# Seven of eight experts put in order of their token count, with their sort moved forward, and more warming products at the start

## The chip, the cores and the metric

The kernel runs on one core of a Trainium2 chip. The metric is the device time of one execution in microseconds. Before the change three runs took 249.92, 250.83 and 251.06 us, so the median is 250.83 us.

The core has a matrix engine (PE, with its weight loads shown apart as PEld), a vector engine (DVE), a scalar engine (ACT), GpSimd (POOL, which also issues the indirect DMAs that gather and scatter rows) and a queue for direct DMAs (SP). Each engine works through its own list of instructions in order; the lists wait for one another through semaphores.

## The reference

A Mamba-2 scan is followed by a mixture of experts with one expert per token. Cut to what matters:

```python
# scan: 4 batches x 8 heads, 768 tokens, head_dim 32, d_state 16, chunks
y_intra = einsum((C B^T) * exp(cum_i - cum_j) * causal, x)
y_inter = einsum(C, state) * exp(cum)
state   = decay_full * state + sum_j B_j x_j exp(cum_last - cum_j)

x = attn_out.transpose(0, 2, 1, 3).reshape(3072, 256)
expert_idx = argmax(cosine(x, expert_emb) / tau)      # 8 experts
gate_w     = softmax(...)[expert_idx]
for e in range(8):                                    # w1: 256 x 1024, w2: 1024 x 256
    mask = expert_idx == e
    out[mask] = gate_w[mask] * (relu(x[mask] @ w1[e]) @ w2[e])
```

Everything is fp32. With the given inputs the eight experts receive 408, 348, 366, 396, 382, 354, 405 and 413 tokens, in this order of expert numbers (counted from the reference).

## The kernel before, in words

**The scan.** The sequence is cut into six chunks of 128 tokens (`NC`), each with all four batches and eight heads. `mamba` writes the order of all instructions out by hand (`manual_schedule`). Ahead of its loop stand the loads of the first chunks, constants, and products of a matrix of ones whose result nobody reads (`warm_up`). In chunk 0 and 1 the PE does, in turn, `inner` (L401), `outputs` (L439), `first_outputs` (L452), `sums` (L369) and `spread_decays` (L215); ACT keeps the outputs (`keep_outputs`, L464). The finished rows of each chunk, with their eight router scores, are sent to a table in HBM, `y_rows`.

**Routing.** `pick`, `count_picks`, `rank_rows` and `places` give every token its expert and its rank among that expert's tokens. `locate` (L743) turns this into sums over chunks, and `table` (L764, L766) turns the sums into a table of token numbers: for each of the eight experts four columns (`NT`) of 104 rows (`TR`), so at most 416 tokens. `from_rows` (L791) makes the indices `gi` for the gathers, `to_rows` with `out_rows` (L799, L1085 to L1095) the rows `to` for the scatters.

**Experts in order of count.** Every expert is a `Job`. The number of token columns that its products work on is fixed when the kernel is built. The first `FIXED` = 2 experts, numbers 0 and 1, have the full 416. The other six (`SORTED`) are put in order of their counts by `sort_experts`, some sixteen DVE instructions (L809 to L839, then L791 to L1095), and the i-th of them gets `CAPS[i]` columns: 416, 408, 400, 388, 376, 364. Tokens above a job's columns would be done by a loop at the end (`leftover`), which is skipped when there are none. Since the order is known only on the chip, `load_weights` reads the number of the expert from `k.order` into a register of SP (L94) for a sorted expert, and issues five DMAs: four for `w1` (L85) and one for `w2` (L105). Tiles for weights exist three times (`wp`, bufs=3).

**Between scan and experts** (`scan_end`). Expert 0 is done in two halves of 208 columns. The first half (`first`) holds tokens of the first three chunks and is gathered early, while the scan still runs; its eight steps `up(0)` to `up(7)` and the two `down` fill the PE while the routing of the last chunk is done on DVE. The second half is `late`, expert 1 is `whole`. `whole` gets its first two gathered tiles from an early table `gi0` and the other two from `gi`. `late` and `whole` share the tile `next_x` (six parts), and `Gates` squares their rows (ACT, L1417), takes a root on POOL (`power`, L1423) and makes the gate weights.

**The experts** (`moe`). From expert 1 on, `up_blocks` and `down_blocks` do the two products with one level of a Winograd scheme: 28 matmuls each (seven products of half-sized blocks, L1272 and L1344), each over half of the job's columns. The sums of blocks of weights (`sum_w1` L1229, `sum_w2` L1237) and of inputs (L1241) are on DVE. Between the two, the next job's rows are transposed (`turn_x`, L1171). The last job has `up_blocks` but plain `down` products (`moe_end`, L1202): 16 over a fixed half of 208 columns, 16 over the rest. Everything is a list per engine; a wait of one engine moves all that stands behind it.

The lines that the change touches most:

```python
def load_weights(k, e, parts=(0, 1), after=None):
    if e >= FIXED:
        i = bass.ds(nc.values_load(k.order[0:1, e - FIXED : e - FIXED + 1], engines=(SP,), ...), 1)
```

Of the kernel before, what the change touches and what calls it, by code (L numbers as in the profile page):

```python
# [17 lines left out]
Q = 128  # L18
# [5 lines left out]
KD, KF = DM // 128, F // 128  # L24
TR, NT = 104, 4
CAP = TR * NT
FIXED = 2
SORTED = E - FIXED
CAPS = [CAP - 8 * i - 4 * max(i - 2, 0) for i in range(SORTED)]
LEFT = (T - CAPS[-1]) // Q + E  # L30
# [594 lines left out]
def place_consts(k):  # L625
    nc, ints = k.nc, k.ints
    k.place_at = ints("place_at", [128, TR], [[1, TR]], 1, 0)
    k.first_of = ints("first_of", [128, NT], [[TR, NT]], 0, 0)
    k.idx_t = k.mc.tile([128, TR], F32, name="idx_t")
    k.same = k.mc.tile([128, E * NT], F32, name="same")  # L630
    nc.gpsimd.tensor_copy(out=k.same[:], in_=k.ident[:, 0:32])
    for b in range(1, NB):
        nc.gpsimd.tensor_tensor(
            out=k.same[:], in0=k.same[:], in1=k.ident[:, 32 * b : 32 * b + 32], op=ALU.add
        )
    k.minus = k.mc.tile([128, 1], F32, name="minus")
    nc.gpsimd.memset(k.minus[:], -1.0)
    k.shifted = k.mc.tile([128, E], F32, name="shifted")
    nc.gpsimd.memset(k.shifted[:], 0.0)
    nc.gpsimd.memset(k.shifted[0:1, 0:2], 1.0)  # L640


def pick(k, c):
# [123 lines left out]
    return t  # L767


def end_places(k, whole):  # L770
    nc = k.nc
    n = k.pz[1][:, 456 : 456 + E]
    nc.tensor.matmul(n, lhsT=k.ones[:], rhs=k.pre[:, NU, :], start=True, stop=True)
    t = table(k)
    k.gi = k.const.tile([TR, E * NT], I32, name="gi")
    k.to = k.const.tile([TR, E * NT], I32, name="to")
    from_rows(k, t[:, 0 : FIXED * NT], 0)
    late = late_job(k)
    gather_tiles(k, whole.x[:, HT:], k.gi, NT + HT)
    nc.vector.tensor_copy(out=k.idx[:], in_=t)  # L780
    idx = k.idx[:, 0 : FIXED * NT]
    to_rows(k, idx, 0)
    late.to, whole.to = k.to[:, HT:NT], k.to[:, NT : 2 * NT]
    k.n = k.const.tile([128, E], F32, name="n")
    nc.vector.tensor_copy(out=k.n[:], in_=n)
    return late


# [55 lines left out]
def mamba(k):  # L844
    nc = k.nc
    k.f = k.mc.tile([128, 2, Q], F32, name="f")
    k.fe = k.mc.tile([128, 2, 3], F32, name="fe")
    k.rT = k.mc.tile([128, 2, 2, 128], F32, name="rT")
    k.V = k.mc.tile([128, NB, 2 * D], F32, name="V")
    k.ends = k.mc.tile([128, 8, NB, 3], F32, name="ends")  # L850
    k.rr, k.wm = {}, {}
    for c in range(NC):
        k.ld[c] = Net()
        k.ld[c].g = []
    load_decays(k)
    expert_emb(k)
    load(k, 0, ("ct", "bi", "x"))
    build_consts(k)
    warm_up(k, 12)
    decays(k)  # L860
    load(k, 1, ("ct",))
    load(k, 0, ("b", "xa"))
    load(k, 1, ("bi", "x", "xa", "b"))
    square_emb(k)
    clear_first_half(k, 0)
    clear_first_half(k, 1)
    route_consts(k)
    spread_decays(k, 0)
    spread_decays(k, 1, [t[:, 384:512] for t in k.py + k.pz])
    warm_up(k, 1, 384)  # L870
    split_b(k, 0)
    inverses(k, 0, 0)
    scale_c(k, 0)
    inverses(k, 0, 1)
    block_ends(k)
    scale_emb(k)
    inner(k, 0, 0)
    mask_inner(k, 0, 0)
    turn_inverses(k, 0, k.py[0][:, 0:256])
    scale_x(k, 0, nc.gpsimd)  # L880
    scale_first_half(k, 0, nc.gpsimd)
    spread_ends(k, k.pz[0][:, 0:96])
    turn_emb(k, k.py[0][:, 256:272])
    scale_c(k, 1)
    steps = between(k, 1, NC)
    next(steps)

    for c in range(NC):
        t = k.ld[c]
        n = c + 1  # L890
        if c == 0:
            load(k, 2, ("ct", "x", "xa", "b", "bi"))
        elif c + 2 < NC:
            load(k, c + 2, ("x",))
        if 2 <= c < NC - 1:
            spread_decays(k, n)
        if 2 <= c < NC - 1:
            add_sums(k, c)
        if c >= 2:
            inner(k, c, 0)  # L900
        if c == NC - 1:
            finish(k, c - 1, (0,))
            early_places(k, c - 3)
        if c >= 2:
            mask_inner(k, c, 0)
        if c == NC - 2:
            load_first_w1(k, 0, t.masked)
        if c > 0 and c + 2 < NC:
            load(k, c + 2, ("ct",), t.masked if c >= 2 else None)
        if 3 <= c < NC - 1:  # L910
            finish(k, c - 1, (0,))
            locate(k, c - 3)
            keep_located(k, c - 3)
        if n < NC:
            scale_x(k, n, nc.gpsimd, t.paired if c >= 2 else None)
        if 1 <= c < NC - 1:
            scale_c(k, n)
        if c == 1:
            decay_states(k, 1)
            add_sums(k, c)  # L920
        if c >= 2:
            pick(k, c - 2)
        if c > 0:
            finish(k, c - 1, (2,) if c == NC - 1 else (1, 2) if 3 <= c else (0, 1, 2))
            keep_rows(k, c - 1)
            if c < NC - 1:
                send_rows(k, c - 1)
        inner(k, c, 1)
        mask_inner(k, c, 1)
        if c > 0 and n < NC:  # L930
            decay_states(k, n)
        if c > 0 and c + 2 < NC:
            load(k, c + 2, ("bi", "xa"), t.masked)
        if c == 0:
            sums(k, 0)
        if n < NC:
            split_b(k, n)
            mask_c(k, n)
            if c == 0:
                next(steps)  # L940
            pass_c(k, n)
        if c == NC - 1:
            k.early_x = half_rows(k)
            gather_tiles(k, k.early_x, k.gi0, 0, 3 * NB * Q)
        if c >= 2:
            count_picks(k, c - 2)
        if c == NC - 1:
            add_located(k, c - 3)
        if c == 0:
            scale_first_half(k, n, nc.gpsimd, (0,))  # L950
        elif n < NC:
            scale_first_half(k, n, nc.gpsimd, after=t.paired)
        if 3 <= c < NC - 1:
            add_located(k, c - 3)
        if c > 0:
            from_states(k, c)
        if c >= 2:
            rank_rows(k, c - 2)
            keep_ranks(k, c - 2)
        outputs(k, c, 0)  # L960
        if c == 0:
            inner(k, 1, 0)
            add_sums(k, 0)
            mask_inner(k, 1, 0)
        first_outputs(k, c, 0)
        for zs in ((0,), (1,)) if c == NC - 1 else (range(KD),):
            outputs(k, c, 1, zs)
            if c == 0:
                spread_decays(k, 2)
            first_outputs(k, c, 1, zs)  # L970
            keep_outputs(k, c, zs)
        if c > 0 and c + 2 < NC:
            load(k, c + 2, ("b",), t.kept)
        if c == NC - 2:
            load_first_w1(k, 1, t.kept)
        if c == NC - 1:
            hold(k, send_rows(k, c - 1), t.kept)
            load_weights(k, 0, (1,), t.kept)
        if c + 2 < NC:
            sums(k, n)  # L980
        if c == 2:
            turn_inverses(k, 1, k.pz[0][:, 0:256])
        if c == NC - 1:
            pick(k, c - 1)
            count_picks(k, c - 1)
        if c >= 2:
            places(k, c - 2)
        if c == 4:
            shift_places(k)
        if c == 1:  # L990
            inverses(k, 1, 0)
            inverses(k, 1, 1)
        if c == 0:
            scale_first_half(k, n, nc.gpsimd, (1,))
            place_consts(k)


def scan_end(k):
# [9 lines left out]
    pick(k, c)  # L1008
    count_picks(k, c)
    whole = whole_job(k)  # L1010
    gather_tiles(k, whole.x[:, 0:HT], k.gi0, NT, 3 * NB * Q)
    for f in range(3):
        first.up(f)
    rank_rows(k, c)
# [5 lines left out]
    gates.square(0)  # L1020
    first.up(4)
    gates.square(1)
    gates.power()
    for f in (5, 6, 7):
        first.up(f)
    locate(k, c, False, True)
    first.down(0, fs=range(1))
    late = end_places(k, whole)
    first.down(0, fs=range(1, KF))
    gates.largest()  # L1030
    gates.scale()
    gates.exp()
    first.gate = gates.end()
    first.to = k.to[:, 0:HT]
    k.gates = Gates(k, k.ep, k.next_x, TR, HT + NT)
    for i in (2, 3):
        k.gates.square(i)
    sort_experts(k)
    first.down(1, fs=range(6))
    late.turn_x()  # L1040
    first.down(1, fs=range(6, KF))
    load_weights(k, 1, (0, 1), late.turned)
    late.w2, whole.w1, whole.w2 = k.w2t[0], k.w1t[1], k.w2t[1]
    load_weights(k, FIXED)
    k.step = k.ints("step", [128, LEFT], [[1, LEFT]], 0, 0)
    k.part = k.ints("part", [128, 1], [[0, 1]], 0, 1)
    return first, late, whole
# [20 lines left out]
def gather_tiles(k, x, gi, at, rows=T):  # L1068
    for i in range(HT):
        gather(k, x[:, i, 0:W], gi[:, at + i : at + i + 1], rows)  # L1070
# [385 lines left out]
def moe(k, early, late, whole):  # L1456
# [10 lines left out]
    for f in range(KF):  # L1467
        late.up(f)
        if 1 <= f <= HT:
            last.out(f - 1)  # L1470
        if 1 <= f < 5:
            gates.square((0, 1, 4, 5)[f - 1])
    gates.power()
    e += 1
    jobs.append(begin(e))
# [314 lines left out]
```

## Time and profile before

| | before |
|---|---|
| runs, median | 250.83 us |
| profiled execution, device time | 252.85 us |
| its span, first to last instruction | 250.8 us |
| mean granted PE clock over the span | 0.971 |
| PE busy | 239.4 us (95%) |
| DVE busy | 181.3 us (72%) |
| ACT busy | 126.1 us (50%) |
| POOL busy | 123.1 us (49%) |

The profiled execution is 2.0 us longer than its span and 2.02 us longer than the median of the three plain runs. In the timeline rows further down the columns are: start in us, duration of the group in us, engine, line, operation, output and input, count, and in square brackets the idle time of the engine before it with what ended it. An fp32 matmul is recorded as two instructions, so `x8` is four matmuls. Where a row has two durations of overlapping instructions, the difference of start times says more than the duration.

### The profile page before, as it was taken

How to read it: one execution, taken by the hardware profiler on the slowest of the kernel's cores; microseconds unless marked ns; L12 is line 12 of the kernel's file. 1: busy time of each engine (PE TensorE's matmuls, PEld its weight loads, DVE VectorE, ACT ScalarE, POOL GpSimd, SP SyncE). 2: the span in 40 equal slices, each digit the busy share in tenths (PEclk: the TensorE clock that was granted, in tenths of full speed). 3: DMA queues.
4: the chain of work that ended last, by engine and by line, in shares of the span. 5: the costliest groups of instructions: out<-in, count | busy, mean ns of one | idle time of the engine just before them, and what ended most of it. 6: DMA issues, size and time to landing. Idle time of an engine off the chain costs nothing.

```text
span 250.8 us, 6978 instructions
## 1 busy us (share of the span) xinstructions
PE 239.4 (95%) x2672; PEld 218.6 (87%) x2672; DVE 181.3 (72%) x479; ACT 126.1 (50%) x363; POOL 123.1 (49%) x161
## 2 busy tenths in 40 slices
PE   6699999999999999999999999999999999999990
PEld 2587878878789899999999999989999999999990
DVE  6854689889774638778969878897987986884121
ACT  3442766884253542653683295266348528428300
POOL 5896364463526583731375177248417527026033
PEclk9857999999999999999999999999999999999996
DMA  3994476665193499996922952492195201001001
GB/s 124 289 266 160 153 255 198 193 176 127 38 290 104 125 278 247 269 272 168 267 58 55 218 186 63 112 257 78 38 260 152 63 0 54 11 0 51 14 18 41
DMA packets 22547, 35.91 MB, mean 143 GB/s; under 512 B 2777, under 2 KB 15780, under 8 KB 22512
## 3 DMA queue, kind: packets, MB, share of 16 engines
q1 hardware_dynamic: 19264, 28.73, 41.6%
q0 software_dynamic: 3088, 6.67, 9.7%
q8 instruction: 21, 0.34, 0.6%
q14 instruction: 14, 0.11, 0.1%
q10 hardware_dynamic: 160, 0.06, 0.1%
HBM read 29.05 MB, written 6.50 MB: 142 GB/s over the span
## 4 chain that ended last, share of the span: by engine, by line
PE 73%; issue 9%; DMA 8%; ACT 3%; POOL 2%; SPq 2%; DVE 1%; POOLq 1%; ACTq 0%
PE yp L1344 19%; PE yp L1272 13%; PE hp L1272 9%; DMA out_dram<-yo,to 5%; PE pg L401 4%; PE py L452 3%; PE py L439 3%; DMA bi<-in_BT_dram 3%; PE hp L1184 2%; PE yp L1202 2%; PE py L422 2%; PE yp L1171 2%; POOL out_dram L1395 2%; PE eb L1184 2%; PE pz L469 1%
## 5 line engine op out<-in xcount | busy, mean ns | idle before, releaser
L1395 POOL DMA_INDIRECT out_dram<-yo,to x32 | 34.4, 1074 | 60.0 <-ACT yo L1392 42.3
L1074 POOL DMA_INDIRECT xg<-y_rows,gi x26 | 31.8, 1224 | 11.5 <-issue 6.9
L411 DVE TENSOR_TENSOR g<-pg,mask 128x1536 f32<-128x1536 f32 x12 | 21.1, 1757 | 10.0 <-PE pg L401 9.9
L1290 ACT ACTIVATE hT<-hT 128x416 f32<-128x416 f32 (+5 forms) x42 | 22.4, 535 | 11.0 <-DVE hT L1294 8.2
L1344 PE MATMUL yp<-T,S 128*128 128x208 f32 (+4 forms) x144 | 26.4, 333 | 0.0
L1294 DVE TENSOR_TENSOR hT<-hp,u 128x416 f32<-128x416 f32 (+5 forms) x28 | 15.7, 567 | 13.8 <-PE hp L1272 6.7
L1344 PEld LDWEIGHTS yp<-T,S 128*128 128x128 f32 x144 | 24.6, 190 | 0.0
L1272 PE MATMUL yp<-T,S 128*128 128x208 f32 (+5 forms) x112 | 21.3, 333 | 0.2 <-ACT u L1285 0.2
L1423 POOL TENSOR_TENSOR gr<-gr,half 104x4 f32<-104x4 f32 (+2 forms) x8 | 9.7, 1214 | 22.9 <-ACT sq L1417 22.9
L1285 ACT COPY p<-yp 128x416 f32<-128x416 f32 (+5 forms) x14 | 6.7, 481 | 27.7 <-PE yp L1272 27.7
L1272 PEld LDWEIGHTS yp<-T,S 128*128 128x128 f32 x112 | 18.3, 190 | 0.6 <-ACT u L1285 0.6
L1344 PE MATMUL yp<-hT,w 128*128 128x208 f32 (+4 forms) x96 | 18.2, 333 | 0.0
L1202 PE MATMUL yp<-hT,w 128*128 128x208 f32 (+1 forms) x96 | 16.4, 326 | 0.3 <-PEq L1627 0.3
L313 POOL TENSOR_TENSOR xs<-x,rT 128x1024 f32<-128x1024 f32 x6 | 12.1, 2008 | 9.2 <-issue 5.7
L1344 PEld LDWEIGHTS yp<-hT,w 128*128 128x128 f32 x96 | 16.5, 190 | 0.0
L1202 PEld LDWEIGHTS yp<-hT,w 128*128 128x128 f32 x96 | 15.6, 190 | 0.5 <-ACT hT L1327 0.5
L1285 ACT COPY u<-yp 128x416 f32<-128x416 f32 (+5 forms) x28 | 13.6, 489 | 2.8 <-PE yp L1272 2.3
L1241 DVE TENSOR_TENSOR T<-hT 128x832 f32<-128x832 f32 (+4 forms) x12 | 11.9, 990 | 3.6 <-ACT hT L1290 3.0
L464 ACT COPY yT<-py 128x512 f32<-128x512 f32 x12 | 6.5, 588 | 12.5 <-PE py L452 12.5
L401 PE MATMUL pg<-cp,bi 32*128 32x128 f32 x192 | 12.4, 326 | 0.0
L1229 DVE TENSOR_TENSOR S<-w 128x512 f32<-128x512 f32 x14 | 9.6, 683 | 3.7 <-DMA w<-in_moe_w_dram 3.7
L401 PE MATMUL pg<-cp,bt 32*128 32x64 f32 x192 | 10.7, 284 | 1.5 <-DVE cp L282 0.9
(308 smaller groups left out, 594.6 us busy)
## 6 DMA issues: line engine op xcount, KB each, us to landing
w<-in_moe_w_dram SPq DMA_DIRECT2D x32, 256.0 KB
w<-in_moe_w_dram SPq DMA_DIRECT2D x8, 1024.0 KB
y_rows<-rows SPq DMA_DIRECT2D x6, 528.0 KB
x<-in_x_dram SPq DMA_DIRECT2D x6, 512.0 KB
ct<-in_CT_dram SPq DMA_DIRECT2D x6, 256.0 KB
bi<-in_BT_dram SPq DMA_DIRECT2D x6, 256.0 KB
b<-in_B_dram SPq DMA_DIRECT2D x6, 256.0 KB
xa<-in_x_dram SPq DMA_DIRECT2D x6, 128.0 KB
```

Source lines behind the costliest of these rows:

```text
L313: d = engine.tensor_tensor(out=t.xs[:].rearrange("p b (h d) -> p b h d", h=NH), in0=t.x[:].rearrange("p b (h d) -> p b h d", h=NH), in1=r_ ...
L401: t.paired = k.nc.tensor.matmul(k.pg[:, q, 192 * u + a : 192 * u + a + n], lhsT=m, rhs=x, start=True, stop=True, tile_position=(32 * q, 0),)
L411: t.masked = k.nc.vector.tensor_tensor(out=g[:], in0=k.pg[:, :, 0:384].rearrange("p q (u m) -> p q u m", u=2), in1=k.mask[:].unsqueeze(1). ...
L1074: k.nc.gpsimd.indirect_dma_start(out=x, out_offset=None, in_=k.y_d[0:rows, :], in_offset=bass.IndirectOffsetOnAxis(ap=at, axis=0), bounds_ ...
L1202: nc.tensor.matmul(t, lhsT=s.w2[:, f, 128 * j : 128 * j + 128], rhs=s.hT[:, f, r], start=(f == order[0]), stop=(f == order[-1]),)
L1241: s.k.nc.vector.tensor_tensor(out=T[n], in0=x, in1=y, op=ALU.subtract)
L1272: nc.tensor.matmul(t[:, m * u : m * u + m], lhsT=w[:, f : f + 128], rhs=x, start=start and u == 0, stop=True, skip_group_check=True,)
L1285: nc.scalar.copy(out=p[:, 0 : 2 * m], in_=t[:, 0 : 2 * m])
L1290: nc.scalar.activation(h, h, ACT.Relu)
L1294: nc.vector.tensor_tensor(out=h, in0=view(t), in1=view(p), op=ALU.add)
L1344: nc.tensor.matmul(t, lhsT=a[:, f], rhs=b[:, f], start=start and f == 0, stop=(f == 3), skip_group_check=True)
L1395: d = nc.gpsimd.indirect_dma_start(out=k.out[:, :], out_offset=bass.IndirectOffsetOnAxis(ap=s.to[:p, i : i + 1], axis=0), in_=y[:p], in_of ...
```

## The change

`FIXED` goes from 2 to 1, so `SORTED` is 7 and `CAPS` becomes 416, 408, 400, 388, 376, 364, 352. Expert 0 alone keeps a fixed place. With that:

- the job `whole` is now the largest of the other seven. Its four tiles can be gathered only with the sorted table, so the two gathers from `gi0` are gone and two more stand behind the sort; its weights are addressed by `k.order`, and the register is loaded before they are issued.
- `sort_experts` moves from behind the gate weights of the first half to right behind the table, ahead of `to_rows` and of the gates; `gates.power()` on POOL moves behind the gathers of `late`.
- the last part of the table is located behind `up(5)` instead of `up(7)`; the table itself stands behind `up(6)`.
- all six squares for `late` and `whole` are done in the loop over `late.up` (before: two ahead of it, four in it).
- `warm_up` has 15 products of 512 columns instead of 12, then 4 of 384 instead of 1, and 2 new ones of 384 ahead of `scale_c(1)`.
- in chunk 0, `first_outputs` stands ahead of `spread_decays(2)`.

```diff
-FIXED = 2
+FIXED = 1
 SORTED = E - FIXED
 CAPS = [CAP - 8 * i - 4 * max(i - 2, 0) for i in range(SORTED)]
...
-    nc.gpsimd.memset(k.shifted[0:1, 0:2], 1.0)
+    nc.gpsimd.memset(k.shifted[0:1, 0:FIXED], 1.0)
...
-def end_places(k, whole):
+def end_places(k, whole, gates):
...
     from_rows(k, t[:, 0 : FIXED * NT], 0)
     late = late_job(k)
-    gather_tiles(k, whole.x[:, HT:], k.gi, NT + HT)
     nc.vector.tensor_copy(out=k.idx[:], in_=t)
-    idx = k.idx[:, 0 : FIXED * NT]
-    to_rows(k, idx, 0)
-    late.to, whole.to = k.to[:, HT:NT], k.to[:, NT : 2 * NT]
     k.n = k.const.tile([128, E], F32, name="n")
     nc.vector.tensor_copy(out=k.n[:], in_=n)
+    gates.power()
+    sort_experts(k)
+    gather_tiles(k, whole.x[:, 0:HT], k.gi, NT)
+    gather_tiles(k, whole.x[:, HT:], k.gi, NT + HT)
+    to_rows(k, k.idx[:, 0 : FIXED * NT], 0)
+    late.to, whole.to = k.to[:, HT:NT], k.to[:, NT : 2 * NT]
     return late
...
-    warm_up(k, 12)
+    warm_up(k, 15)
...
     spread_decays(k, 1, [t[:, 384:512] for t in k.py + k.pz])
-    warm_up(k, 1, 384)
+    warm_up(k, 4, 384)
...
     turn_emb(k, k.py[0][:, 256:272])
+    warm_up(k, 2, 384)
     scale_c(k, 1)
...
             outputs(k, c, 1, zs)
+            first_outputs(k, c, 1, zs)
             if c == 0:
                 spread_decays(k, 2)
-            first_outputs(k, c, 1, zs)
             keep_outputs(k, c, zs)
...
     whole = whole_job(k)
-    gather_tiles(k, whole.x[:, 0:HT], k.gi0, NT, 3 * NB * Q)
     for f in range(3):
         first.up(f)
...
     gates.square(1)
-    gates.power()
-    for f in (5, 6, 7):
-        first.up(f)
+    first.up(5)
     locate(k, c, False, True)
-    first.down(0, fs=range(1))
-    late = end_places(k, whole)
-    first.down(0, fs=range(1, KF))
+    first.up(6)
+    late = end_places(k, whole, gates)
+    first.up(7)
+    first.down(0)
     gates.largest()
     gates.scale()
     gates.exp()
     first.gate = gates.end()
     first.to = k.to[:, 0:HT]
     k.gates = Gates(k, k.ep, k.next_x, TR, HT + NT)
-    for i in (2, 3):
-        k.gates.square(i)
-    sort_experts(k)
     first.down(1, fs=range(6))
     late.turn_x()
     first.down(1, fs=range(6, KF))
     load_weights(k, 1, (0, 1), late.turned)
     late.w2, whole.w1, whole.w2 = k.w2t[0], k.w1t[1], k.w2t[1]
-    load_weights(k, FIXED)
+    load_weights(k, 2)
...
-        if 1 <= f < 5:
-            gates.square((0, 1, 4, 5)[f - 1])
+        if 1 <= f <= HT + NT:
+            gates.square(f - 1)
```

## The prediction

> **What bounds the kernel now.** I read the page's slices first, then the chain of waits, then the timeline of PE, DVE, POOL and SP around three places.
>
> ```profile
> PE   6699999999999999999999999999999999999990
> PEclk9857999999999999999999999999999999999996
> PE 73%; issue 9%; DMA 8%; ACT 3%; POOL 2%; SPq 2%; DVE 1%; POOLq 1%; ACTq 0%
> ```
>
> PE is full from the fourth slice to the last, and the chain that ends last is PE for 73%. From about 70 us on the end moves with the PE's own work and with what makes PE wait. The second row shows the exception at the start: slices 2 to 4 have a lower clock.
>
> **Part 1: fewer columns.** What an expert costs is read from equal groups of four matmuls in jobs of different size (timeline of PE; four groups of L1272 and two of L1171):
>
> ```profile
> 121.59 1.57 PE L1272 MATMUL yp<-T,S 128*128 128x208 f32 x8
> 123.00 0.38 PE L1389 MATMUL ot<-ident,yoT 128*104 128x128 f32 x2
> ...
> 226.49 1.40 PE L1272 MATMUL yp<-T,S 128*128 128x182 f32 x8
> 227.72 0.38 PE L1389 MATMUL ot<-ident,yoT 128*104 128x128 f32 x2
> ...
> 173.61 0.84 PE L1171 MATMUL yp<-ident,xg 104*128 104x104 f32 x8
> 174.29 1.56 PE L1344 MATMUL yp<-hT,S 128*128 128x200 f32 x8
> ...
> 194.24 1.25 PE L1171 MATMUL yp<-ident,xg 104*128 104x104 f32 x8
> 195.42 1.58 PE L1344 MATMUL yp<-hT,S 128*128 128x194 f32 x8
> ```
>
> Start to next start: 1.41 us with 208 columns, 1.23 with 182, so 0.0069 us per column and group by these two rows; between the 208- and 188-column jobs it is 1.41 to 1.28, or 0.0065. A job has 14 such groups (56 matmuls). Before, jobs 1 to 7 have 416, 416, 408, 400, 388, 376, 364 columns; after, 416, 408, 400, 388, 376, 364, 352. Of the six jobs with both block products one of 416 becomes one of 364: 14 x (1.405 - 1.235) = 2.38. The last job: seven groups, 182 to 176 columns: 7 x 6 x 0.0065 = 0.27; and sixteen plain products (four groups) with 144 instead of 156: 4 x 12 x 0.0065 = 0.31. Transposes: the eight instructions of L1171 take 0.71 us with a last tile of 104 rows and 0.67 with one of 76, so a 104-row tile that becomes one of 40 saves about 0.15 (estimate). But the last two rows above show a step: with a last tile of 76 rows (173.61 to 174.29) the turn takes 0.68, with one of 64 rows 1.18, and the turn at 214.67 with 52 rows 1.17. No wait is named for it. Two jobs have this step now; the sizes 64, 52 and 40 make it three: +0.47. Sum: 2.38 + 0.27 + 0.31 + 0.15 - 0.47 = **-2.64**. Bounds: -3.1 if the step is of another cause and stays at two, -2.0 if DVE, whose sums of weights do not shrink, starts to hold PE (it is 18.4 of 21.6 us busy in the job from 161 us, where PE already loses some 0.8 us around 166 to 169 to ACT and DVE).
>
> The new caps hold: 413, 405, 396, 382, 366, 354, 348 tokens against 416 to 352 leave 3 to 10 free, so the leftover loop stays empty.
>
> **Part 2: the table earlier.** Before, the last part is located at 77.37, the table's sum follows:
>
> ```profile
> 75.39 0.29 DVE L733 TENSOR_TENSOR eq<-eq,tok 128x128 f32<-128x128 f32 x1
> 77.89 0.26 DVE L764 TENSOR_TENSOR idx_t<-idx_t,pz 128x104 f32<-128x104 f32 x1 [2.21 <-PE pz L743]
> 78.61 0.17 DVE L791 TENSOR_SCALAR gi<-pz 104x8 int32<-104x8 f32 x1 [0.46 <-PE pz L766]
> 79.10 1.14 POOL L1074 DMA_INDIRECT next_x<-y_rows,gi  x1 [1.54 <-DVE idx L780]
> 80.54 2.88 DMA next_x<-y_rows,gi
> 83.47 0.49 PE eb L1171 x3
> ```
>
> DVE has its operands ready at 75.68, and waits 2.21 us for PE. After, PE does `up(4)` and `up(5)` from 74.36 (8 instructions of 0.176 each) and locates at 75.8, 1.6 earlier; the sum (L764) is done at 76.55, under `up(6)` (0.7), which ends at 76.8; table at 77.0, `gi` at 77.25, the two gathers of `late` at 77.75 and 79.2: 1.35 earlier. The second lands at 79.2 + 2.88 = 82.05. Today PE reaches the transposes at 83.07 and needs 0.72 for four of them that take 0.36 elsewhere (eight in 0.71): it waits for this landing. That is 0.36, and two gaps of 0.05 at 78.0 to 78.4: **-0.46**. Next late is then the copy of these transposes on ACT (0.51), as today.
>
> **Part 3: the sort ahead, two gathers moved.** The sort runs from 82.13 to 84.50 (`gi`) today, 2.37 us; with 49 and 196 elements instead of 36 and 144 I take 2.6 (the largest pair, 0.41 and 0.30, grows by a third). After: 77.6 to 80.2, `order` at 79.1. Behind it on DVE: its own `to` (1.1, to 81.3), `to` of expert 0 (1.1, to 82.4), the gates of the first half (0.35 + 0.55, to 83.3). Waiting for these: ACT's exp at 83.4, in front of the copy of `late`'s transposes (83.65). It fits by 0.1; if DVE is 0.5 later, PE loses 0.3. POOL: gathers for `late` to 80.3, `power` 0.75 to 81.05, then four gathers for `whole` at 1.4 each, 81.1 to 86.4, landing by 88.5; the four small instructions that follow (0.8) end at 87.2, ahead of the scatter at 87.42 today. `whole` is squared from 87.5 on and transposed at 93.4: 5 us of cover, without which each us late is a us of PE. The sixth square moves from 89.3 to about 90.5, so `power` to about 92.3, still ahead of its reader behind the next row.
>
> ```profile
> 84.97 1.74 SPq L85 DMA_DIRECT2D w<-in_moe_w_dram  x4
> 88.03 2.16 SPq L85 DMA_DIRECT2D w<-in_moe_w_dram  x4
> ...
> 92.17 0.69 DVE L1229 TENSOR_TENSOR S<-w 128x512 f32<-128x512 f32 x1 [3.71 <-DMA w<-in_moe_w_dram]
> ```
>
> The weights of `whole` are issued when `late`'s transposes are copied (84.64), and DVE waits for them until 92.17. After, SP first loads a register from `order`, ready at 79.1, so the release, now about 84.2, decides. With an address from a register four issues take 2.16 instead of 1.74 (second row against first): +0.4. Two more gathers (110 KB each: 104 rows x 264 x 4 bytes) move beside these weights, at the 215 GB/s or so of that stretch another 1.0. So the wait ends at about 93.1, not 91.7. Behind it on DVE stand two sums (1.4), the gates' `scale` (0.8), the copies of `xT` (1.1 for both), which PE needs at 96.9. PE waits only if the weights come after about 93.6, and the later operations (`yoT`, transposed at 98.3) are 0.1 to 0.3 short. I take **+0.1** (0 to +1.0). The moved squares lie in ACT's idle time.
>
> **Part 4: the start.** Warming products first, in the 1.14 us (5.68 to 6.82), 0.93 us and 0.47 us that PE stands idle there.
>
> ```profile
> 7.84:11.25 3.41, 2.50 (x44) 2.35 (x44) 2.79 (x7) 1.23 (x5) 2.62 (x12) 1.00 0.89 285
> 11.25:14.66 3.41, 2.94 (x66) 2.65 (x68) 2.26 (x7) 2.21 (x8) 3.33 (x3) 0.50 1.04 282
> 18.08:21.49 3.41, 3.41 (x72) 2.90 (x70) 2.35 (x3) 0.00 (x0) 2.90 (x13) 0.50 0.95 314
> 15.85 2.09 PE pg L401 x32
> 30.79 0.89 PE pg L401 x32
> ```
>
> (Busy time by stretch, PE first, the clock third from the end; then two pieces of the chain.) The clock is 0.50 from 11.25 to 21.49, after a stretch in which PE had instructions in flight for 2.50 of 3.41 us. The Trainium skill, "TensorE: Matmul & The Clock Gate", section "Why this matters for your kernels", says the clock is kept while PE has no idle gap above about 3 us. By it no drop was due here, and more products in gaps of at most 1.14 us would be worth nothing. The row disagrees: the longest gap was 1.14 and the clock fell. So it is fullness that counts, and I estimate it: the matmuls of that stretch need about 1.0 us of streaming (30%), from the full-clock rates above. Three products of 384 columns add up to 0.48 (512 columns at full clock are 384/512 of some 0.21 us each, since twelve take 4.18 with the first at half clock). That gives 37% to 45%; a stretch around 21.5 to 25 that I put at 48% kept its clock. The threshold lies between, I cannot say where.
>
> If the clock holds: from 15.85 (set by the load of `bi` until 12.73 and four ACT steps, which no clock changes) the pieces up to 21.6 take 0.99 + 0.61 + 0.58 + 0.61 + 0.43 + 0.58 instead of 2.09 + 1.05 + 1.01 + 0.86 + 0.74 + 0.65: 2.6 less, of which I take **-2.35**, since DVE and POOL keep their pace. If it falls as before, the two last products cost 0.17 at 11.8, under the wait for ACT: 0. Swapping `spread_decays` and `first_outputs` frees the ACT copy 0.74 earlier, but PE is full except for 0.16 at 22.7: **-0.15** in both cases.
>
> **Rivals and numbers.** The profiled execution (252.85) is 0.8% above the median; the differences are taken as they are.
>
> - A, likeliest, 0.50: the clock falls as before (the warming does not do what it is for). -2.64 - 0.46 + 0.1 - 0.15 = -3.15, so **247.7** (profiled: span 247.7). Own range 246.9 to 248.9. For it: 37 to 45% is nearer to the 30% that fell.
> - B, 0.33: the clock holds. -3.15 - 2.35 = -5.5: 245.3. For it: the added products sit in the very stretch. Against: I know the threshold only within 30 to 48%, and the plain runs may not all drop today.
> - C, 0.13: weights or gates of Part 3 come 1.5 to 2.5 us late, or DVE holds PE in the smaller jobs: 249.2 to 250.5.
> - D, 0.04, slower: the register and the gathers put the first sorted weights far back. Place: DVE at L1229. It decides once that wait ends beyond 93.6 + 3.2 + 1.25 = about 98, that is 13 us after issue where 7.2 are needed now: then 252.5. Nothing in the transfers speaks for half the rate.
>
> About 0.5% (1.25 us) is what a measurement can tell from no change. C gives 0.07 below 249.6 and 0.06 within. Faster 0.90, same 0.06, slower 0.04. Range: 245.0 (B with the full size of Part 1) to 249.4 (half of C).
>
> **What would show it.** Right: groups of eight in the last job 1.20 apart; `gi` near 77.2 and no wait ahead of the transposes of `late` (less the shift of the start); first gather of `whole` near 81; L1229 released at 92 to 93.5; three turns of 1.2 us; tail unchanged. The clock row tells A from B, and L401 at 15.85 with 0.99 or 2.09. Wrong: a gap on PE between 84 and 100 above 0.5 us, the clock low in a later stretch, or PE groups waiting for DVE in jobs 4 to 7.

## The result, and the profile after

| | before | after |
|---|---|---|
| profiled execution | 252.85 us | 247.81 us |
| its span | 250.8 us | 246.0 us |
| mean granted PE clock | 0.971 | 0.996 |

The ratio of the times, after to before, is 0.9873, with a 95% interval of 0.9825 to 0.9921: 3.2 us less on 250.8, or **247.6**; the profiled run and the fastest one had 247.81 and 247.05 us. Two more runs of the changed kernel took 252.66 and 253.10 us: the ratio leaves them out, and over all four runs the median is 250.24 us, against 250.75 before. The experiments show one cause in the change itself that can lengthen a run by 3 to 4 us; whether it acted in these two is not shown.

The page's slices and the chain's shares by engine:

```profile
PE   7989999999999999999999999999999999999990
PEclk9999999999999999999999999999999999999998
PE 69%; issue 11%; DMA 7%; ACT 4%; DVE 4%; POOL 2%; SPq 2%; POOLq 1%; DVEq 0%; ACTq 0%
```

The dip of the clock in slices 2 to 4 is gone. PE stays the bound. For the profiled span, case A of the prediction had 247.7 us and case B 245.3; 246.0 was measured. To see where the 4.8 us between the two spans come from, I compare the start times of the same groups on PE in the two timelines (worked out from start to start):

| stretch | before | after | difference |
|---|---|---|---|
| to the first `up` of `first` | 70.13 | 66.98 | -3.15 |
| from there to the first product of `whole` | 27.18 | 27.40 | +0.22 |
| the six jobs with both block products | 126.27 | 124.96 | -1.31 |
| the last job, to its last transposes | 21.30 | 20.69 | -0.61 |
| the tail behind them | 5.92 | 5.97 | +0.05 |

**The start.** Busy time by stretch, for the three stretches of the prediction (PE first, the clock third from the end):

```profile
7.84:11.25 3.41, 2.97 (x48) 2.46 (x46) 2.79 (x7) 1.32 (x5) 2.88 (x12) 1.00 1.00 354
11.25:14.66 3.41, 2.53 (x98) 1.92 (x96) 3.17 (x8) 3.30 (x11) 3.33 (x3) 1.00 0.87 280
18.08:21.49 3.41, 3.05 (x68) 2.19 (x68) 1.88 (x6) 1.35 (x4) 2.90 (x13) 1.00 0.93 323
```

Pieces of the chain of waits after (start, duration, what), and behind them a row of PE's timeline in e4_turn76:

```profile
5.89 5.60 DMA bi<-in_BT_dram
...
14.76 1.17 PE pg L401 x32
...
18.57 0.57 issue
19.14 0.43 DVE T L359
19.66 0.86 DVE V L385 x4
...
15.81 0.45 PE L401 MATMUL pg<-cp,bt 32*128 32x64 f32 x8 [0.94 <-ACT cp L307]
```

The clock is 1.00 in all three, and L401 takes 1.17 us where it took 2.09. The load of `bi`, ahead of L401, was shorter too: 5.60 us, where the profile before had 6.84. That is not the change's, but it explains little. e4_turn76 below has the same start, and `bi` lands there as late as before, so that its L401 begins at 15.81 (last row; 15.85 before); its first `up` still stands at 67.33, which is 2.80 us earlier than before. In e1_warm_only, whose chain does not pass through `bi`, it is 2.98. So about 0.2 to 0.35 of the 3.15 us belong to this run and not to the change. With the faster PE a new wait shows at 18.57 to 20.5, for DVE's `V`: a faster PE finds the next limit.

**Between scan and experts.** Rows picked from the timelines of POOL, DVE, PE, ACT and SP, in order of time, and behind them two of PE before:

```profile
74.35 0.16 DVE L793 TENSOR_SCALAR gi<-pz 104x4 int32<-104x4 f32 x1 [0.75 <-PE pz L766]
74.99 1.10 POOL L1072 DMA_INDIRECT next_x<-y_rows,gi  x1 [4.40 <-DVE key L811]
77.16 0.51 DVE L793 TENSOR_SCALAR gi<-sorted_idx 104x28 int32<-104x28 f32 x1
79.86 0.52 PE L1169 MATMUL eb<-ident,next_x 104*128 104x104 f32 x4
80.94 0.21 ACT L1443 ACTIVATE gl<-gl 104x16 f32<-104x16 f32 x1 [2.66 <-DVE gr L1437]
81.06 0.49 ACT L1172 COPY xT<-eb 128x416 f32<-128x416 f32 x1
81.58 1.96 SPq L85 DMA_DIRECT2D w<-in_moe_w_dram  x4
81.60 1.67 PE L1182 MATMUL hp<-xT,w 128*128 128x208 f32 x8 [0.50 <-issue]
...
87.86 3.13 PE L1200 MATMUL yp<-hT,w 128*128 128x208 f32 x16
89.62 0.20 DVE L1428 TENSOR_REDUCE gm<-next_x 104x6 f32<-104x48 f32 x1 [4.59 <-DMA next_x<-y_rows,gi]
90.03 0.69 DVE L1227 TENSOR_TENSOR S<-w 128x512 f32<-128x512 f32 x1
90.82 0.88 PE L1169 MATMUL yp<-ident,next_x 104*128 104x104 f32 x8
...
90.94 2.98 PE L1202 MATMUL yp<-hT,w 128*128 128x208 f32 x16
93.76 0.88 PE L1171 MATMUL yp<-ident,next_x 104*128 104x104 f32 x8
```

Counted from the first `up`, `gi` stands at 7.37 us instead of 8.48, and the four transposes of `late` (L1169) no longer wait. Then PE loses 0.50 us ahead of `late.up`, because the copy of these transposes stands on ACT behind an exp that waits 2.66 us for DVE. Further down, DVE goes straight from the gathered rows (89.62) to the first sum of weights (90.03): it waits for the gathers now, not for the weights. And the first `down` of `late` on PE (L1200, then the transposes of `whole`) takes 87.86 to 90.82, or 2.96 us, where it took 2.82 before (90.94 to 93.76); why is told with the experiments.

**The experts.** The stall in the fourth block job, the turn in front of the last job, and groups of eight in the last job; then the same stall in the kernel before:

```profile
164.13 1.72 PE L1270 MATMUL yp<-T,S 128*128 128x194 f32 x8 [0.15 <-ACT u L1283]
166.02 1.58 PE L1270 MATMUL yp<-T,w 128*128 128x194 f32 x8 [0.17 <-issue]
...
210.69 1.22 PE L1169 MATMUL yp<-ident,xg 104*128 104x104 f32 x8
211.83 1.50 PE L1342 MATMUL yp<-hT,S 128*128 128x182 f32 x8
...
222.16 1.36 PE L1270 MATMUL yp<-T,S 128*128 128x176 f32 x8
223.36 0.38 PE L1387 MATMUL ot<-ident,yoT 128*104 128x128 f32 x2
...
167.53 1.76 PE L1272 MATMUL yp<-T,S 128*128 128x200 f32 x8 [0.15 <-ACT u L1285]
169.45 1.62 PE L1272 MATMUL yp<-T,w 128*128 128x200 f32 x8 [0.16 <-issue]
```

The groups are 1.20 us apart with 176 columns, as forecast; three turns are long (1.14 to 1.19 us); the stall at 164 to 167, which stood in the fourth block job before (167 to 170), is there again: these two groups are 1.89 us apart, as against 1.92.

### The profile page after: what moved, and what is told of

The parts are those of the page before. It is cut to its first block, busy times and chain, and to the rows that moved or that the text cites. A ratio compares the mean times of both kernels' runs of the same rounds, so it can differ in the third digit from the quotient of the medians.

```text
span 246.0 us, 7006 instructions
## 1 busy us (share of the span) xinstructions
PE 235.1 (96%) x2680; PEld 213.0 (87%) x2680; DVE 181.0 (74%) x479; ACT 124.8 (51%) x363; POOL 123.6 (50%) x161
## 4 chain that ended last, share of the span: by engine, by line
PE 69%; issue 11%; DMA 7%; ACT 4%; DVE 4%; POOL 2%; SPq 2%; POOLq 1%; DVEq 0%; ACTq 0%
PE yp L1342 19%; PE yp L1270 10%; PE hp L1270 7%; DMA out_dram<-yo,to 5%; PE pg L401 4%; PE py L452 3%; PE py L439 3%; PE hp L1182 2%; PE yp L1200 2%; PE eb L1200 2%; DMA bi<-in_BT_dram 2%; PE py L422 2%; PE yp L1169 2%; PE eb L1182 2%; POOL out_dram L1393 2%
## 5 line engine op out<-in xcount | busy, mean ns | idle before, releaser
L1288 ACT ACTIVATE hT<-hT 128x416 f32<-128x416 f32 (+6 forms) x42 | 22.0, 528 | 10.9 <-DVE hT L1292 7.4
L1342 PE MATMUL yp<-T,S 128*128 128x208 f32 (+5 forms) x144 | 25.8, 329 | 0.0
L1292 DVE TENSOR_TENSOR hT<-hp,u 128x416 f32<-128x416 f32 (+6 forms) x28 | 15.4, 558 | 13.5 <-PE hp L1270 4.4
L1270 PE MATMUL yp<-T,S 128*128 128x208 f32 (+6 forms) x112 | 20.9, 330 | 0.2 <-ACT u L1283 0.2
L1283 ACT COPY p<-yp 128x416 f32<-128x416 f32 (+6 forms) x14 | 6.6, 474 | 26.3 <-PE yp L1270 26.3
L1342 PE MATMUL yp<-hT,w 128*128 128x208 f32 (+5 forms) x96 | 17.9, 329 | 0.0
L1200 PE MATMUL yp<-hT,w 128*128 128x208 f32 (+1 forms) x96 | 16.2, 323 | 0.3 <-PEq L1625 0.3
L1200 PEld LDWEIGHTS yp<-hT,w 128*128 128x128 f32 x96 | 15.2, 190 | 0.7 <-ACT hT L1325 0.5
L1283 ACT COPY u<-yp 128x416 f32<-128x416 f32 (+6 forms) x28 | 13.3, 482 | 2.9 <-PE yp L1270 2.4
L1239 DVE TENSOR_TENSOR T<-hT 128x832 f32<-128x832 f32 (+5 forms) x12 | 11.7, 972 | 3.6 <-ACT hT L1288 2.4
L1239 DVE TENSOR_TENSOR T<-hT,T 128x832 f32<-128x832 f32 (+5 forms) x12 | 11.7, 972 | 0.2
L1270 PE MATMUL yp<-T,w 128*128 128x208 f32 (+6 forms) x56 | 11.1, 340 | 0.5 <-issue 0.4
L401 PE MATMUL pg<-cp,bt 32*128 32x64 f32 x192 | 9.9, 262 | 1.4 <-ACT cp L307 0.9
```

What stands on the lines that cost most here:

```text
L401: t.paired = k.nc.tensor.matmul(k.pg[:, q, 192 * u + a : 192 * u + a + n], lhsT=m, rhs=x, start=True, stop=True, tile_position=(32 * q, 0),)
L1200: nc.tensor.matmul(t, lhsT=s.w2[:, f, 128 * j : 128 * j + 128], rhs=s.hT[:, f, r], start=(f == order[0]), stop=(f == order[-1]),)
L1239: s.k.nc.vector.tensor_tensor(out=T[n], in0=x, in1=y, op=ALU.subtract)
L1270: nc.tensor.matmul(t[:, m * u : m * u + m], lhsT=w[:, f : f + 128], rhs=x, start=start and u == 0, stop=True, skip_group_check=True,)
L1283: nc.scalar.copy(out=p[:, 0 : 2 * m], in_=t[:, 0 : 2 * m])
L1288: nc.scalar.activation(h, h, ACT.Relu)
```

## The experiments

Each ratio is to the kernel before, in runs on the same chip (e1 to e4 on one chip, e5 to e12 on another); times 250.8 it gives us. Where two intervals overlap, the ratios alone do not put the two kernels in order.

| run | what differs | ratio | 95% interval |
|---|---|---|---|
| after | | 0.9873 | 0.9825 to 0.9921 |
| e3_old_caps | after, without the smaller columns | 0.9995 | 0.9962 to 1.0027 |
| e1_warm_only | before, with the warming products | 0.9976 | 0.9949 to 1.0003 |
| e2_old_start | after, with the old start | 0.9847 | 0.9783 to 0.9912 |
| e7_sixth_step | before, locating at the sixth step | 0.9983 | 0.9950 to 1.0016 |
| e4_turn76 | after, at least 76 rows in a turn | 0.9811 | 0.9749 to 0.9872 |
| e5_gates_first | e4, gates ahead of `to_rows` | 0.9864 | 0.9800 to 0.9928 |
| e6_weights_later | e4, weights of `whole` two steps later | 0.9825 | 0.9770 to 0.9880 |
| e9_hold_f0 | e4, these weights one step later | 0.9805 | 0.9756 to 0.9854 |
| e10_gates_hold | e5 and e9 | 0.9872 | 0.9818 to 0.9927 |
| e12_spread_only | e4, leftover steps spread | 0.9832 | 0.9780 to 0.9883 |
| e8_all | e5, leftover spread, 12 first products | 0.9849 | 0.9785 to 0.9912 |
| e11_all_hold | e8 and e9 | 0.9797 | 0.9740 to 0.9855 |

### The columns alone

```diff
-CAPS = [CAP - 8 * i - 4 * max(i - 2, 0) for i in range(SORTED)]
+CAPS = [CAP] + [CAP - 8 * i - 4 * max(i - 2, 0) for i in range(SORTED - 1)]
```

> The changed kernel with the column counts of before (416, 416, 408, 400, 388, 376, 364 for the seven sorted experts), everything else changed. Theory 'columns': 2.6 us slower than the changed kernel (the sum of part 1: 2.38 + 0.27 + 0.31 + 0.15 - 0.47), so about 0.6 us faster than before. Theory 'clock': less than 1 us slower than the changed kernel. In the profile two turns of L1169 take 1.2 us instead of three.

Measured 0.9995: with every other part of the change in place and the old columns, no gain is left that these runs can tell from zero. By the two ratios the columns are worth 0.0122 x 250.8 = 3.1 us, by their intervals 1 to 5; the ratio of the changed kernel rests on two runs, and some runs of e3 may carry the late landing that is shown next. The fastest runs of the two differ by 1.75 us (248.80 and 247.05). In the traces the seven jobs give 1.31 + 0.61 = 1.92, and the six block jobs of e3 take 126.25 us, as before (126.27). So the columns are the main part of the gain, but by the traces nearer to 2 us than to 3, and what makes up the rest of the 3.2 is not shown; why that is less than 2.64 is told below.

The profiled run of e3 took 253.51 us and shows what a late landing of the gathers does (timeline of ACT and PE):

```profile
91.80 0.42 ACT L1415 ACTIVATE sq<-next_x 104x256 f32<-104x256 f32 x1 [1.92 <-DMA next_x<-y_rows,gi]
92.59 0.77 PE L1200 MATMUL yp<-hT,w 128*128 128x208 f32 x2 [2.04 <-ACT hT L1186]
```

Busy time by stretch, PE first, the clock third from the end:

```profile
89.50:92.90 3.40, 1.18 (x6) 0.61 (x5) 1.02 (x3) 1.13 (x6) 0.50 (x1) 1.00 1.13 321
92.90:96.30 3.40, 3.40 (x15) 3.25 (x14) 2.74 (x9) 0.57 (x2) 2.87 (x3) 0.50 1.05 245
```

The sixth square waits for its gather. Behind it on ACT stands the relu of the last step of `late` (L1186), and PE needs that relu for the last two matmul records of a `down`: 2.04 us idle. PE is busy for 1.18 of 3.40 us there, and right behind it the clock is 0.50 for a stretch of 3.4 us. From the first `up` to the first product of `whole` this run takes 31.25 us, where the changed kernel, which has the same instructions up to there, took 27.40. So the forecast's "5 us of cover", counted to the transposes of `whole`, was counted to the wrong reader; the relu comes earlier.

### The start

e1 is the kernel before with `warm_up(k, 15)`, `(4, 384)` and the two new products of 384; e2 is the kernel after with `(12)` and `(1, 384)`, no new ones, and the old order of `first_outputs`.

> The kernel before with the warming products alone (15, 4 and 2). Theory 'columns': the plain runs of before lose little to the clock, so the time stays within 0.5 us of before. Theory 'clock': the warming carries most of the gain of the full change, 2.2 to 2.6 us faster than before, and the profile shows the clock at full from about 5 us on. If the clock falls in spite of the products, as forecast A had it: no change and a row of 0.5 between about 11 and 21 us.

> The changed kernel with the start of before (12 and 1 warming products, none ahead of scale_c(1), spread_decays ahead of first_outputs). Theory 'columns': 2.5 to 3.2 us faster than before, as the full change. Theory 'clock': at most 1 us faster than before, since the columns are given back by the half microsecond that PE stands idle ahead of late.up and by later waits.

e1 had a mean clock of 0.99 or more in 19 of 22 runs (median 250.09), and never below 0.98. The kernel before, beside it, had that in 17 of 43 runs (median 249.76); 18 runs were below 0.98 (median 252.32). So three things hold at once. The products do keep the clock up. A fallen clock costs 252.32 - 249.76 = 2.6 us, near the 2.35 of the forecast. And yet the gain by the ratio is small, 0.0024 x 250.8 = 0.6 us, as the clock before did not fall in every run (the medians over all 22 and all 43 runs are 250.14 and 251.00, 0.9 apart), and as the longer warming has a price: in the chain of e1

```profile
1.50 5.55 PE pz L181 x15
7.05 0.53 PE pg L215 x8
```

the fifteen products end at 7.05 us, past the 6.82 at which `spread_decays` could start before. e2, without all of it, is within the interval of the changed kernel (0.9847), though its profile has a clock of 0.5 and 0.8 in two slices. By the ratios, then, the start is worth nothing that these runs can tell from zero, though it changes how often the clock falls. It is no full guarantee either: in the profile of e5, which has all the products, the clock falls to 0.5 in the third slice.

### The table at the sixth step

> The kernel before with one edit: the last part of the table located behind up(5) and the table behind up(6). Part 2 of the forecast gives 0.46 us less than before: gi 1.35 us earlier, the four transposes of late in 0.36 instead of 0.72. Rival: PE only waits elsewhere (the copy of the transposes, the relus), and the first L1184 of late moves by less than 0.2.

Measured -0.4 us, with 1 inside the interval. In its timeline `gi` stands 7.73 us behind the first `up` (8.48 before), but the first gather of `late` is issued 1.58 us after `gi` starts, where before it was 0.49, and the transposes still wait:

```profile
76.97 1.14 POOL L1074 DMA_INDIRECT next_x<-y_rows,gi  x1 [1.89 <-DVE gm L1430]
81.31 0.49 PE L1171 MATMUL eb<-ident,next_x 104*128 104x104 f32 x3 [0.16 <-DMA next_x<-y_rows,gi]
```

The profile names a DVE instruction of the gates as the releaser; why the gather would need it is open. The gain at the transposes needs the order of the changed kernel on POOL and DVE (`power` behind the gathers, sort ahead of gates) as well.

### The step of the turn

```diff
-o, p = (j - j0) * m + i * tr, s.tile_rows(i)
+o, p = (j - j0) * m + i * tr, max(s.tile_rows(i), min(tr, 76))
```

> The changed kernel, in which the transposes of a job's last tile take at least 76 rows (surplus rows are not read). If the half microsecond by which three turns are longer belongs to last tiles of 64 rows and fewer: the three turns of L1169 fall from 1.14 to 1.2 us to about 0.7 and the kernel is 1.3 to 1.5 us faster than the changed one. If it belongs to a wait in the smaller jobs (DVE or ACT late): no change of the turns beyond 0.1, the kernel 0 to 0.2 us slower from the added columns.

The same turn as in the changed kernel, with 76 rows of the last tile transposed, of which 36 are never used:

```profile
209.67 0.84 PE L1169 MATMUL yp<-ident,xg 104*128 104x104 f32 x8
210.35 1.44 PE L1342 MATMUL yp<-hT,S 128*128 128x182 f32 x8
```

It takes 0.68 us instead of 1.14. All three turns do, 1.47 us in all, and the ratio falls by 0.0062 (1.6 us), though the intervals overlap; the turns themselves are shown by the trace. More rows are faster: the step at 64 rows and fewer belongs to the rows, and three jobs of the changed kernel pay it. Why it is there is open.

### Gathers and weights on the same transfers

e5 puts the gates of the first half ahead of both `to_rows` on DVE, so that the exp in front of `late`'s copy isn't late.

> The changed kernel with 76-row turns, and the gates of the first half ahead of both to_rows on DVE. If the half microsecond in which PE stands idle ahead of late.up comes from ACT's exp, which waits for DVE behind eleven to_rows instructions: late.up follows the last down(1) matmul without a gap, 0.4 to 0.5 us less than e4_turn76 from the first L1182 of first to the first of late. If it comes from the landing of late's gathers: the gap stays.

The gap of 0.50 us ahead of `late.up` is gone (from the first `up` to there 13.99 us, 14.63 in e4), and yet the ratio is higher than that of e4, with overlapping intervals. In its profile, a run of 253.19 us, two squares wait for gathers (2.13 and 1.69 us), PE stands 1.81 us behind a relu and the clock is 0.7 in that slice. The copy is earlier, so the weights of `whole`, which are issued behind it, are too, and the gathers land later. e6 turns this round:

```diff
-    load_weights(k, 1, (0, 1), late.turned)
...
+        if f == 1:                      # in the loop over late.up
+            load_weights(k, 1, (0, 1), late.relu)
```

> The changed kernel with 76-row turns, and the weights of whole issued behind the second relu of late.up instead of behind the copy of late's transposes, some 2 us later. If the last two gathers of whole land late (5.7 us after POOL is done with the last one, in the changed kernel) because they share the transfers with these weights: they land within 3 us of their issue, the wait of DVE L1428 ends 2 us or more earlier, and ACT's sixth square waits for nothing; the time is the same or up to 0.5 us less, and runs above 252 us become fewer. If the gathers are late by themselves: nothing moves, and DVE L1227 waits for the weights instead.

```profile
87.97 0.20 DVE L1426 TENSOR_REDUCE gm<-next_x 104x6 f32<-104x48 f32 x1 [1.98 <-DMA next_x<-y_rows,gi]
92.27 0.69 DVE L1225 TENSOR_TENSOR S<-w 128x512 f32<-128x512 f32 x1 [3.85 <-DMA w<-in_moe_w_dram]
...
97.38 0.32 PE L1385 MATMUL ot<-ident,yoT 128*104 128x128 f32 x1 [0.51 <-DVE yoT L1207]
```

Now the gathers are in time and the weights are the late ones: DVE waits 3.85 us, and PE loses 0.51 at `yoT`, which is just the chain that the forecast had written down for late weights. e9 takes the step between (`f == 0`), e10 the same with the gates of e5.

> The changed kernel with 76 rows at least in a turn, and the weights of `whole` issued behind the first relu of `late` (in the kernel of e6_weights_later it was the second). Theory 1 (gathers and weights share the transfers): issue comes about 0.7 to 1.4 us later than in e4_turn76 (81.93 there in its own span, so near 83), the gathers land 3.1 to 5 us after POOL's last issue, the sums at the first w1 sum on DVE wait until about 91.5 instead of 92.3, and the idle time of PE at 97 (0.51 in e6) is gone: about 0.5 us below e6, that is ratio 0.980 to 0.982, with fewer runs above 250. Rival 2 (the moment of issue does not matter, landing varies by itself): ratio as e4 (0.981) and the same share of slow runs, one in five or six.

> The kernel of e5_gates_first (gates of the first half ahead of both rows of scatter targets), and the weights of `whole` issued behind the first relu of `late`. Theory 1: the gap ahead of late.up is gone (0.5 us) and the weights no longer stand in front of the gathers, so PE waits for no square at 96: ratio 0.978 to 0.981, about 0.4 below e9. Rival 2 (the half-clock stretch of e5 came from the gates' order and not from the weights): PE still stands 1.8 us at 96 and the clock falls behind it, ratio 0.986 as e5.

The profiles of all these kernels give one series: SP's first issue of these weights against the end of POOL's last gather issue, the start of the DVE reduction that reads all gathered rows, and the length of the first `down` of `late` on PE, whose last matmuls wait for the relu behind the sixth square:

| kernel | weights issued, against the last gather's issue | rows there, after that issue | first `down` of `late` |
|---|---|---|---|
| e6 | 0.23 us earlier | 3.1 us | 2.81 us |
| e9 | 0.95 earlier | 4.2 | 2.81 |
| e10, e11 | 1.6 earlier | 5.7, 5.8 | 3.58, 3.73 |
| e12 | 2.35 earlier | 5.4 | 2.81 |
| after, e4, e2 | 2.35 earlier | 5.7, 5.8, 5.9 | 2.96, 3.06, 3.16 |
| e5, e3, e8 | 2.96 to 3.12 earlier | 7.3 to 7.8 | 5.2 to 5.7 |

From e4 over e9 to e6 only the weights move, and the landing moves with them: it is the weights' load, and not the gates' order, that delays the gathers. Each row is one profile, and between 1.6 and 2.35 us the series does not order the landings. The last column shows where the cover ends: at 5.4 us PE loses nothing, at 5.7 to 5.9 it loses 0.15 to 0.35, one tenth for each tenth, and at 7.3 and more 2 us and then half clock. So the profiled run of the changed kernel already lies just beyond the edge. e3 has the same instructions up to there; in its profile the weights start 0.6 us sooner against the gathers, and from the first `up` to `whole` it takes 3.85 us more. (In e10 and e11 PE arrives 0.6 us earlier, as its gap is gone, and so loses more at the same landing.)

Whether the runs at 252.66 and 253.10 were of this kind is not shown: they carry no trace, they lie over 5 us above the other two, and single long runs occur with the weights held as well (e6 251.34, e11 252.86). In e9 PE waits for neither weights nor gathers, and its six runs lie between 245.66 and 248.14. e10 fell short of what was expected: with the gates first, the relu that releases the weights comes earlier too, so it lost most of the hold; besides, its sixth product of `whole` comes 1.5 us late, with no wait named.

### The stall in the fourth block job

```diff
-        for _ in range(3):
+        for _ in range(3 if i < 3 else 2 if i < 5 else 1):
```

> The kernel of e4_turn76 with the leftover's steps spread over five jobs (3,3,2,2,1 in place of 3,3,3,2 and so on until they are used up). Theory 1 (the stall of PE in the job of 194 columns, some 0.5 to 0.7 us around 165, comes from the leftover's steps on DVE that delay the sums there): groups from L1270 in that job stay near 1.30 apart, ratio 0.979, 0.5 us below e4. Rival 2 (DVE's own sums of weights are what holds PE): the stall stays or moves one job on, ratio 0.981.

The groups that lay 1.89 us apart in the changed kernel (164.13 to 166.02) are at an even pace:

```profile
165.21 1.48 PE L1270 MATMUL yp<-T,S 128*128 128x194 f32 x8
166.66 1.58 PE L1270 MATMUL yp<-T,w 128*128 128x194 f32 x8
```

That job takes 20.23 us from start to start, against 21.09 in e4, and the next 19.80 against 19.94: the stall came from the DVE steps of `leftover`, three in a row per job. In the changed kernel six of their instructions of 0.40 us each stand ahead of a DVE sum that a relu on ACT waits 1.96 us for, and the copies that PE needs stand behind this relu. In the time of the whole kernel it is not shown: `whole` took 21.65 us in this run, 21.03 in e4, and the ratios overlap.

> e5_gates_first with 12 instead of 15 first warming products (4 and 2 later ones kept), and the leftover bookkeeping on DVE spread over the jobs (3, 3, 2, 2, 1 steps instead of 3 each). If three more first products delay the start where the clock rises late, and if the stall of 0.8 us in the fourth job is DVE's bookkeeping: 0.4 + 0.8 us less than e5_gates_first, so about 245. If the start is set by the load of bi, and the stall by ACT: no difference.

> The kernel of e8_all (e5, 12 first products, leftover steps spread 3,3,2,2,1 over the jobs) with the weights held as in e10. Theory 1: the stall in the job of 194 columns stays away (0.5 us), the start is 0.2 to 0.4 shorter with 12 products, no square is waited for: about 0.8 below e10, ratio 0.975 to 0.978, near 244.8. Rival 2: with 12 products the clock rises late or falls in some runs, and the gain of the spread is lost there: ratio as e10, with a mean clock of 0.98 in the profile.

e8 removes the stall too, but as a child of e5 it has late gathers (PE idle 1.92 us); what its 12 first products do cannot be read, as the clock falls in the fourth slice of its profile. e11, with the weights held, has the lowest ratio of all, 0.9797, though PE still waits 0.64 us for the relu in its profile and one of its runs took 252.86. e9 (0.9805) needs fewer edits than e11 and had no run above 248.14; between e4, e9 and e11 the intervals decide nothing. All three have lower ratios than the changed kernel, but their intervals overlap with its own.

## Why the prediction was right, and where its steps were off

The number came from case A, -3.15, and 3.2 us were measured (by the interval 2.0 to 4.4). The columns carried it, as the text had it. That the sum met the number so closely is luck in part: the columns were forecast too large by the traces, the terms around the routing too favourable, and the clock, put at nothing, gave something. Of the text's signs of being wrong two showed faintly: a gap of 0.50 us on PE ahead of `late.up`, and waits of PE in the fourth and fifth block jobs. The terms behind the sum:

- **Columns, forecast -2.64.** By the whole-kernel comparison -3.1 with a wide interval, by the traces -1.92, just beyond the bound of -2.0 that the text gave in case DVE holds PE. The group times were right (1.20 us), and the last job gave 0.61, as forecast (0.58). What is missing lies in the six block jobs. `whole` took 21.35 us instead of 21.03, with no wait named; across the runs it varies from 21.03 to 22.69. The fourth and fifth block jobs lost another 0.2 and 0.1, since PE's waits for ACT and DVE did not shrink with the columns: the fourth took 21.54 us before and 21.67 after, with six columns less in each half and the long turn (0.5). The stall was in the sum of before already, so it is not its 0.86 us (e12 against e4) that are missing, only what it did not give back. The last 0.1 is the transposes: their saving of 0.15 was not seen, as the turns with 52 and 40 rows take 1.17 and 1.14.
- **The step of the turn, +0.47.** Right, and now shown by e4 as one of rows, not of the job.
- **The table, -0.46.** The moves came as written: `gi` 1.11 us earlier (1.35 forecast) and no wait at the transposes, which is the 0.36. "It fits by 0.1; if DVE is 0.5 later, PE loses 0.3" was the weak place. From `key` to `gi` the sort took 2.95 us where 2.6 were forecast; `gi` alone took 0.51 us for 28 elements, where the 24 of the kernel before took 0.18, and the cause is open. With `gi` of the table 0.24 later than forecast as well, ACT's exp came 13.96 us behind the first `up` instead of 13.27, and PE lost 0.50. From `first` to `whole` the sum is +0.22 instead of -0.36. A margin of 0.1 on a queue with over twenty instructions in it was not one.
- **Weights and gathers, +0.1.** The weights did not come late, and rival C's and D's waits for them did not show. The 0.4 for an address from a register is not shown either: the four issues took 1.96 us after and 1.74 before, but 2.14 in e1, where the address is fixed. The step that failed is "landing by 88.5": less the shift of the start (3.15) that is 85.4, and the rows were there at 89.6. The text priced what two more gathers do to the weights; what the weights do to the gathers, it did not.
- **The clock.** A said that it falls as before. In the profile it did not, and in 19 of 22 runs of e1 it did not; rival B was right in mechanism and near in price per drop (2.6 us against 2.35). In the profiles the start gained 3.15, in e1 2.98 and in e4 2.80, where B had 2.35 and 0.15 for the swapped `first_outputs`; no run separates the swap. The measured time is not B's 245.3, probably because runs of the kernel before hold their clock in many cases: beside e1, 17 of 43 did, and the profile with its 0.971 was one of the worse ones. The forecast named this ("the plain runs may not all drop today") without carrying it into the numbers. So the likeliest case hit the number with one wrong statement in it.
- **The Trainium skill's rule** on idle gaps of about 3 us ("TensorE: Matmul & The Clock Gate", "Why this matters for your kernels"): e1 supports the forecast's reading that shorter gaps can cost the clock. Filling gaps of at most 1.14 us raised the share of runs with a mean clock of 0.99 or more from 17 of 43 to 19 of 22.

## What to carry to other kernels

When a gather and a load of weights run side by side, price the delay in both directions, and follow the queue of the engine that waits: the reader that decides may be an instruction *behind* the waiting one (here a relu behind a square). Before a fallen clock in one profile is booked as a gain, see in how many plain runs it falls. Where work shrinks, look whether the engines beside it shrink as well: a wait for fixed DVE work in a job is not given back when the job gets smaller.

## What the runs showed of the hardware

- A turn of eight instructions whose last tile has 64, 52 or 40 rows took 1.14 to 1.19 us; with 76 rows or more it took 0.68 to 0.72 (e4).
- Gathers of 110 KB each were there 3.1 us after the last issue where the weights' load began 0.2 us ahead of it (e6), and 7.3 to 7.8 us where it began 3 us ahead (e3, e5, e8).
- Behind an idle time of 2.04 us on PE, in a stretch of 3.40 us with 1.18 us busy, the clock was 0.50 for 3.4 us (e3); waits of 0.50 and 0.64 us at the same place (e10, e11) left it at 1.00.
